# A decode attention kernel on one core: one 128-row load of keys is issued as six loads of 112, 3, 3, 3, 3 and 4 rows

## Chip, cores and metric

The kernel runs on one core of one Trainium2 chip. The metric is the time of one execution on the device, in microseconds (us), and lower is better. The time before is 1369.47 us, the median of three runs (1368.61 to 1370.11).

## What is computed

Two independent attention blocks are computed for one new token of each of four batches, and their outputs are laid side by side. Block A has 32 query heads that share 8 key and value heads, and looks at the last 2048 positions of its cache. Block B has 32 heads with keys and values of their own, and looks at all 8192 positions. All data are bf16, and the head dimension is 128.

```python
q = (x @ wq).reshape(B, Sq, H, Dh).transpose(0, 2, 1, 3)
scores = einsum("bhqd,bhkd->bhqk", q, k_cache) * (Dh ** -0.5)
p = softmax(scores, axis=-1)
o = einsum("bhqk,bhkd->bhqd", p, v_cache)
out = o.transpose(0, 2, 1, 3).reshape(B, Sq, H * Dh) @ wo
# A: the same, with the last W = 2048 positions and keys repeated 4 times
return concatenate([a, b], axis=-1)
```

Nearly all of the bytes are the keys and values of B: 4 batches x 32 heads x 8192 positions x 128 numbers of 2 bytes, twice, which is 537 MB of the 587 MB that are read in all.

## The kernel before, in words

The work is a list of chunks. The first eight (A, one for each key head) hold 64 tiles of 128 positions each for keys and as many for values. The next 32 (B, `NCA` = 8 to `NC` - 1) hold four heads of one batch: 256 key tiles and 256 value tiles of 128 x 128, that is 8 MB of keys and 8 MB of values a chunk. In SBUF a chunk's keys take 128 partitions of 64 KB each: one partition holds 256 consecutive positions of one head, and tile j is column block j of all partitions.

A chunk of B (`whole_B`) runs so: TensorE transposes eight key tiles at a time (a group g of 0 to 31, `emit_T`), VectorE or ScalarE copies the transposed group out of PSUM, TensorE multiplies it with the queries (`emit_S`), the softmax runs in two halves, and TensorE multiplies the probabilities with the values (`emit_pv`).

All loads but two tiny ones are issued by SyncE's queue (SP), one after another in the order in which `dma_kB`, `dma_vB`, `dma_wos` and their like are called: for each chunk of B the keys, then the values, and every fourth chunk the output weights ahead of them. Ahead of each load SP waits until the buffer that it overwrites has been read: keys for the transposes of the chunk before, values for the value products of the chunk before. `kpieces` and `vpieces` say into how many pieces a chunk's keys and values are cut by columns. The keys of B's first chunk (`ENDK`) come in three pieces of 64, 64 and 128 tiles, into different parts of the buffer: pieces 0 and 1 into the main part, where A's weights lay before, piece 2 into the spare part, which has to wait for A's last keys. Pieces 0 and 1 are each 128 rows (partitions) of 16 KB.

The landings are not waited for by TensorE itself. GpSimd's queue (POOL) waits for each piece's DMA semaphore in order (`land_kB`) and then raises a counter by the number of groups that came in; TensorE waits for that counter ahead of groups 0, 4, 8, 16 and 24 (`QK`, `QC`, `emit_T`). Piece 1 holds groups 8 to 15. Its semaphore belongs to B's first chunk alone.

The text below calls one of the core's 16 DMA engines a **lane**. A transfer is a list of rows; each row is one packet on one lane, and at its end every lane that took part sends one 4-byte packet that raises the semaphore.

Of the kernel before, what the change touches and what calls it, by code (L numbers as in the profile page):

```python
# [13 lines left out]
P = 128  # L14
# [3 lines left out]
NH = 10  # L18
NWO = 2
LATEWO = 2  # L20
LASTWO = 3
NPB = 2
NSM = 2
# [156 lines left out]
def bass_concat_heads__sliding_block_cached__mha_block_cached__decode_kernel(  # L180
# [30 lines left out]
    NCA = Hkv  # L211
# [13 lines left out]
    sch = _Sched()  # L225
    with ExitStack() as es:
# [5 lines left out]
        def ps(name, shape, dt):  # L232
# [72 lines left out]
            waits=["c_onesf", "c_identf"], key="c_ind")  # L305
# [39 lines left out]
        def flat(at, n):  # L345
            return kv[:, at:at + n, :].rearrange("p s x -> p (s x)")
# [4 lines left out]
        def dma_wq(ab, at):  # L351

            waits = take(("wq", ab), at, 2, ("qmm", ab))
            src = WQ[ab].rearrange("(p r) n -> p (r n)", r=KC)
            sch.add_dma("sp", lambda e: e.dma_start(flat(at, 2), src), "d_h%d" % at, waits=waits, key=("wq", ab))
# [4 lines left out]
        def dma_wo(g):  # L360

            src = A_wo[g * 4 * P:(g + 1) * 4 * P, :].rearrange("(p r) n -> p (r n)", r=4)
            slot = wo_slot(g)
            dst = wor[:, slot, :]
            if g == NCA - 1:
                for h, x in enumerate((slice(0, LASTWO * DO), slice(LASTWO * DO, 4 * DO))):
                    sch.add_dma("sp", lambda e, x=x: e.dma_start(dst[:, x], src[:, x]), "d_wos" if h else "d_wo%d" % slot,
                                waits=[] if h else [("fin", g - 2)], key=("wo", g, h))
                return
            sch.add_dma("sp", lambda e: e.dma_start(dst, src), "d_wo%d" % slot,  # L370
                        waits=[("fin", g - 2)] if g >= 2 else [], key=("wo", g))
# [16 lines left out]
        def kpieces(c):  # L388
            return ENDK if c == NCA else QUARTERS if c == NC - 1 else HALVES if c >= NC - NLATE else WHOLE
# [4 lines left out]
        def dma_kB(c):  # L394

            ch = chunks[c]
            src = B_k[ch["b"], 4 * ch["hq"]:4 * ch["hq"] + 4].rearrange("u (pp j) d -> (u pp) (j d)", pp=P // 4)
            pieces = kpieces(c)
            fam = "d_k%d_" % len(pieces)
            s0 = ch["s"] - ch["NG"]  # L400
            j0 = 0
            for i, n in enumerate(pieces):
                spare = len(pieces) > 1 and j0 >= KMAIN
                if spare:
                    dst = kspare[:, (j0 - KMAIN) * P:(j0 - KMAIN + n) * P]
                    waits = held[8] + held[9] if c == NCA else [("T", s0 + (j0 + n) // TG - 1)]
                else:
                    dst = flat(KB, 4)[:, j0 * P:(j0 + n) * P]
                    if c == NCA:
                        waits = held[0] + held[1] + held[2] + held[3]  # L410
                    else:
                        waits = [("T", s0 + min(j0 + n, KMAIN) // TG - 1)]
                        if j0 + n > KMAIN and len(kpieces(c - 1)) == 1:
                            waits += [("cp", c - 1)]
                x = slice(j0 * P, (j0 + n) * P)
                sch.add_dma("sp", lambda e, x=x, dst=dst: e.dma_start(dst, src[:, x]), fam + str(i), waits=waits, key=("k", c, i))
                j0 += n

        def land_kB(c):
# [24 lines left out]
        def dma_vB(c):  # L444

            ch = chunks[c]
            src = B_v[ch["b"], 4 * ch["hq"]:4 * ch["hq"] + 4].rearrange("u (pp j) d -> (u pp) (j d)", pp=P // 4)
            dst = flat(VB, 4)
            pieces = vpieces(c)
            fam = "d_v%d_" % len(pieces)  # L450
            j0 = 0
            for i, n in enumerate(pieces):
                waits = held[4] + held[5] + held[6] + held[7] if c == NCA else [("pv", c - 1, 0 if j0 + n <= NTB // 2 else 1)]
                x = slice(j0 * P, (j0 + n) * P)
                sch.add_dma("sp", lambda e, x=x: e.dma_start(dst[:, x], src[:, x]), fam + str(i), waits=waits, key=("v", c, i))
                j0 += n
# [21 lines left out]
        for c in range(NCA):  # L478
# [3 lines left out]
            if c == 2:  # L482
                dma_wq(1, 6)
            if c != 1 and c < NCA - LATEWO:
                dma_wo(c)
# [3 lines left out]
        for c in range(NCA, NC):  # L489
            if (c - NCA) % NB == 0:  # L490
                dma_wos((c - NCA) // NB)
            dma_kB(c)
            dma_vB(c)
        for c in range(NCA - LATEWO, NCA):
            dma_wo(c)
# [9 lines left out]
        def pe_mm(o, l, r, start=True, stop=True, transpose=False, waits=(), key=None):  # L505
            if transpose:
                sch.add("pe", lambda e: e.transpose(o, l, r), waits, key)  # L507
            else:
                sch.add("pe", lambda e: e.matmul(o, l, r, start=start, stop=stop), waits, key)  # L509
# [348 lines left out]
        def emit_fin(c):  # L858
            ab = 0 if c < NCA else 1
            if ab == 1:  # L860
                ov = oz[:, :].rearrange("p (b u) -> p b u", b=NB)
                ops = [(ov[:, :, u], wol[:, u, :]) for u in range(4)]
                waits = ["c_oz", ("oT", c)]
            else:
                w = wor[:, wo_slot(c), :].rearrange("p (r n) -> p r n", r=4)
                ops = [(zA[:, c % 2, r * NB:(r + 1) * NB], w[:, r, :]) for r in range(4)]
                waits = [("z", c), ("wo", c, 0) if c == NCA - 1 else ("wo", c)]

            for i, (l, r) in enumerate(ops):
                for h, (p0, x) in enumerate(out_halves(ab)):  # L870
                    pe_mm(fin[p0:p0 + NB, 0:DO // 2], l, r[:, x], start=False,
                          stop=i == len(ops) - 1 and c == NCA - 1,
                          waits=waits if i == h == 0 else [("wo", c, 1)] if c == NCA - 1 and (i, h) == (LASTWO, 0) else [],
                          key=("fin", c) if i == len(ops) - 1 and h == 1 else None)
# [172 lines left out]
        for p0, x in out_halves(1):  # L1047
            pe_mm(fin[p0:p0 + NB, 0:DO // 2], zz[:, :], sel4[:, 0:2, :].rearrange("p r x -> p (r x)"), start=False, key=("end", p0))
        for c in range(NCA - LATEWO, NCA - 1):
            emit_fin(c)  # L1050
# [61 lines left out]
```

## Time and profile before

| what | value |
|---|---|
| median of three runs | 1369.47 us |
| the profiled execution, its own time | 1369.16 us |
| span of the profiled execution (first to last instruction) | 1367.4 us |
| busiest engine, PE | 1221.8 us (89% of the span) |
| DMA packets, bytes, mean rate | 16773, 587.52 MB, 430 GB/s |

The profile's parts read as follows. The digits of its second part are busy shares in 40 equal slices of the span, and the GB/s row is what all lanes moved in each slice. The third part gives packets, bytes and busy share of each DMA queue; q1 is the queue of SP's loads, q10 that of ScalarE's (ACT's), q8 and q14 bring program code. The chain of work that ended last goes back from the last instruction: a DMA in it stands for the time from its issue to its landing, its own time in the queue included. A time "from issue to landing" therefore counts the loads ahead of it too.

### The profile page before, as it was taken

What the parts mean: (1) busy time and instruction counts of PE and PEld (TensorE: products, weight loads), DVE (VectorE), ACT (ScalarE), POOL (GpSimd) and SP (SyncE); (2) the same over time, 40 slices, a digit from 0 to 9 for tenths busy, and PEclk for the clock granted to TensorE, in tenths of its full rate; (3) what the DMA queues carried; (4) which work ended last, traced back from release to release, by engine and by line L of the source; (5) the groups of instructions that cost most, each with busy time, mean ns of one, the idle gap of its engine ahead of it and who ended that gap; (6) DMA issues with size and microseconds to landing.
All of it is one profiled execution on the core that took longest, in us unless ns stands there. A gap on an engine that the chain in (4) does not pass through costs nothing.

```text
span 1367.4 us, 62934 instructions
## 1 busy us (share of the span) xinstructions
PE 1221.8 (89%) x27807; PEld 1125.7 (82%) x27843; DVE 731.9 (54%) x1495; ACT 554.9 (41%) x777; POOL 202.8 (15%) x84
## 2 busy tenths in 40 slices
PE   6688799989898999888989899889899989899998
PEld 5587698878887988888889888878898888888888
DVE  3575355545455555454555555545555545455565
ACT  3353244434344443333444344334444333344443
POOL 2000022222210222222101222221012222200000
PEclk9898999999999999999999999999999999999999
DMA  9999999999999999999999999999999999999998
GB/s 399 427 427 429 434 438 429 433 437 418 435 433 435 429 437 429 437 429 437 431 432 433 435 424 435 437 431 431 433 435 433 433 430 439 437 424 430 429 427 370
DMA packets 16773, 587.52 MB, mean 430 GB/s; under 512 B 1880, under 2 KB 2032, under 8 KB 4208
## 3 DMA queue, kind: packets, MB, share of 16 engines
q1 hardware_dynamic: 16720, 587.21, 99.7%
q8 instruction: 15, 0.25, 0.1%
q14 instruction: 6, 0.05, 0.0%
q10 hardware_dynamic: 32, 0.01, 0.0%
HBM read 587.21 MB, written 0.01 MB: 429 GB/s over the span
## 4 chain that ended last, share of the span: by engine, by line
DMA 57%; PE 38%; issue 2%; DVE 2%; ACT 1%; SPq 0%; ACTq 0%; POOLq 0%; DVEq 0%
DMA kv<-in_B_k_cache_dram 51%; PE tr L507 22%; PE sc L509 10%; DMA kv<-in_A_k_cache_dram 4%; PE tr L509 3%; DMA kv<-in_B_v_cache_dram 2%; PE po L509 2%; PE ms L509 1%; DVE kt L584 0%; DVE sA L637 0%; PE fin L509 0%; ACT pba L736 0%; PE sc L940 0%; ACT pbb L706 0%; PE ms L507 0%
## 5 line engine op out<-in xcount | busy, mean ns | idle before, releaser
L507 PE MATMUL tr<-identb,kv 128*128 128x128 bf16 x8704 | 671.9, 223 | 50.0 <-POOLq L83 36.1
L584 DVE COPY kt<-tr 128x1024 bf16<-128x1024 bf16 x736 | 502.7, 691 | 318.9 <-PE tr L507 315.4
L507 PEld LDWEIGHTS tr<-identb,kv 128*128 128x128 bf16 x8704 | 521.0, 100 | 61.8 <-issue 54.3
L582 ACT ACTIVATE kt<-tr 128x1024 bf16<-128x1024 bf16 x352 | 359.3, 1023 | 455.2 <-PE tr L507 452.9
L509 PE MATMUL sc<-qq,kt 128*128 128x64 bf16 x8192 | 400.6, 192 | 11.1 <-DVE kt L584 9.4
L509 PEld LDWEIGHTS sc<-qq,kt 128*128 128x128 bf16 x8192 | 330.3, 98 | 17.7 <-DVE kt L584 12.7
L431 POOL COPY kv<-kv 128x4096 int32<-128x4096 int32 x54 | 192.9, 3602 | 988.6 <-DMA kv<-in_B_k_cache_dram 988.6
L706 ACT ACTIVATE pbb<-sc,negb 32x128 bf16<-32x128 f32 x256 | 137.8, 538 | 134.3 <-DVE negb L688 131.5
L509 PE MATMUL tr<-pbb,kv 128*128 128x64 bf16 x4096 | 135.7, 193 | 28.3 <-ACT pbb L706 25.4
L509 PEld LDWEIGHTS tr<-pbb,kv 128*128 128x128 bf16 x4096 | 131.0, 99 | 32.1 <-issue 30.0
L509 PE MATMUL po<-pbb,kv 128*128 128x64 bf16 x4096 | 135.0, 194 | 4.6 <-issue 4.6
L509 PEld LDWEIGHTS po<-pbb,kv 128*128 128x128 bf16 x4096 | 127.5, 98 | 5.6 <-issue 4.7
L854 ACT ACTIVATE wol<-tr 128x512 bf16<-128x512 f32 x32 | 19.1, 597 | 204.0 <-PE po L509 204.0
L856 DVE CAST wol<-tr 128x512 bf16<-128x512 f32 x64 | 41.2, 686 | 54.9 <-PE tr L509 54.9
L940 PE MATMUL sc<-sel,identb 128*128 128x512 bf16 x167 | 51.0, 384 | 13.5 <-issue 13.5
L940 PEld LDWEIGHTS sc<-sel,identb 128*128 128x128 bf16 x167 | 16.2, 97 | 48.4 <-issue 38.3
L713 DVE TENSOR_REDUCE rs<-pbb 128x4 f32<-128x512 bf16 x32 | 22.0, 686 | 50.0 <-ACT pbb L706 50.0
L786 DVE RECIPROCAL ib<-ms 128x8 f32<-128x8 f32 x32 | 6.6, 208 | 59.4 <-PE ms L509 59.4
L509 PE MATMUL tr<-wos,back 32*128 32x512 bf16 x384 | 34.8, 383 | 0.7 <-issue 0.5
L509 PE MATMUL po<-wos,back 32*128 32x512 bf16 x128 | 33.9, 384 | 0.0
L674 DVE TENSOR_REDUCE gm<-ms 4x4 f32<-4x128 f32 x72 | 19.8, 275 | 25.0 <-PE ms L507 25.0
L654 DVE TENSOR_REDUCE rh<-sc 128x4 f32<-128x512 f32 x32 | 22.1, 692 | 14.3 <-PE sc L509 14.3
(92 smaller groups left out, 505.4 us busy)
## 6 DMA issues: line engine op xcount, KB each, us to landing
kv<-in_B_v_cache_dram SPq DMA_DIRECT2D x10, 4096.0 KB, 24.0
kv<-in_B_k_cache_dram SPq DMA_DIRECT2D x7, 4096.0 KB, 19.7
kv<-in_A_k_cache_dram SPq DMA_DIRECT2D x8, 2048.0 KB, 15.7
kv<-in_A_v_cache_dram SPq DMA_DIRECT2D x8, 2048.0 KB, 16.6
kv<-in_B_k_cache_dram SPq DMA_DIRECT2D x6, 2048.0 KB, 26.2
kv<-in_B_v_cache_dram SPq DMA_DIRECT2D x3, 2048.0 KB, 30.0
kv<-in_A_wq_dram SPq DMA_DIRECT2D x1, 4096.0 KB, 12.3
kv<-in_B_wq_dram SPq DMA_DIRECT2D x1, 4096.0 KB, 23.0
```

Source lines behind the costliest of these rows:

```text
L431: sch.add("pool", lambda e, dst=dst, org=org: e.tensor_copy(dst, org), waits=[("T", s0 + ch["NG"] - 1)] if g == QC[0] else [])
L507: sch.add("pe", lambda e: e.transpose(o, l, r), waits, key)
L509: sch.add("pe", lambda e: e.matmul(o, l, r, start=start, stop=stop), waits, key)
L582: sch.add("act", lambda e: e.activation(dst, src, ACTF.Copy), waits=waits, key=("ev", s))
L584: sch.add("dve", lambda e: e.tensor_copy(dst, src), waits=waits, key=("ev", s))
L654: sch.add("dve", lambda e: e.tensor_reduce(out=dst, in_=src, axis=AX.X, op=ALU.max), waits=[("S", ch["s"] + (half + 1) * ch["NG"] // 2 - 1 ...
L674: sch.add("dve", lambda e: e.tensor_reduce(out=gm[0:C, m, 0:U], in_=src, axis=AX.X, op=ALU.max), waits=[key_of("trm", c, half)], key=key_o ...
L706: sch.add("act", lambda e, src=src, dst=dst, pp=pp, u=u: e.activation(dst, src, ACTF.Exp, bias=negb[pp, half, u:u + 1], scale=scale), wait ...
L713: sch.add("dve", lambda e: e.tensor_reduce(out=dst, in_=probs_of(c, half).rearrange("p j u -> p u j"), axis=AX.X, op=ALU.add), waits=[("ex ...
L854: sch.add("act", lambda e, u=u, o=o: e.activation(wol[:, u, :], o, ACTF.Copy), waits=[("reord", c, u)], key=("wol", c, u))
L856: sch.add("dve", lambda e, u=u, o=o: e.tensor_copy(wol[:, u, :], o), waits=[("reord", c, u)], key=("wol", c, u))
L940: return e.matmul(sc[:, 1, :], identb[:, :], sel4[:, :, :].rearrange("p r x -> p (r x)"), start=True, stop=True)
```

## The change

In `dma_kB`, piece 1 of B's first chunk of keys is no longer one transfer of 128 rows of 16 KB. It becomes six transfers of 112, 3, 3, 3, 3 and 4 rows, which together cover the same rows, source and destination, and are issued one behind the other in its place. The first one has the wait that the single one had; the others have none. All six raise the same semaphore, by 16 each, and the piece counts as landed when it has reached 96 in place of 16.

```diff
+UNEVEN = (112, 3, 3, 3, 3, 4)
...
                 x = slice(j0 * P, (j0 + n) * P)
-                sch.add_dma("sp", lambda e, x=x, dst=dst: e.dma_start(dst, src[:, x]), fam + str(i), waits=waits, key=("k", c, i))
+                r0 = 0
+                for rows in UNEVEN if (c, i) == (NCA, 1) else (P,):
+                    y = slice(r0, r0 + rows)
+                    r0 += rows
+                    sch.add_dma("sp", lambda e, x=x, y=y, dst=dst: e.dma_start(dst[y, :], src[y, x]), fam + str(i), waits=waits, key=("k", c, i) if r0 == P else None)
+                    waits = []
                 j0 += n
```

The one place where instructions move is SP's queue, between B's first output weights and its second chunk of keys. Before, SP issued this (each row is a line of the kernel, the tile written, the tensor read, and rows x elements; L377 are output weights, L416 keys and L455 values):

```order
L377 DMA wos<-in_B_wo_dram 128x2048
L416 DMA kv<-in_B_k_cache_dram 128x8192 x2
L416 DMA kv<-in_B_k_cache_dram 128x16384 [waits eng_pe]
L455 DMA kv<-in_B_v_cache_dram 128x16384 [waits eng_pe]
L455 DMA kv<-in_B_v_cache_dram 128x16384
L416 DMA kv<-in_B_k_cache_dram 128x32768 [waits eng_pe]
```

Now it issues this (the same lines are L378, L421 and L461):

```order
L378 DMA wos<-in_B_wo_dram 128x2048
L421 DMA kv<-in_B_k_cache_dram 128x8192
L421 DMA kv<-in_B_k_cache_dram 112x8192
L421 DMA kv<-in_B_k_cache_dram 3x8192 x4
L421 DMA kv<-in_B_k_cache_dram 4x8192
L421 DMA kv<-in_B_k_cache_dram 128x16384 [waits eng_pe]
L461 DMA kv<-in_B_v_cache_dram 128x16384 [waits eng_pe]
L461 DMA kv<-in_B_v_cache_dram 128x16384
L421 DMA kv<-in_B_k_cache_dram 128x32768 [waits eng_pe]
```

The second of the two 128x8192 loads has become six, all of them ahead of the load that waits for TensorE; every other row stands as it stood, and the other engines' instructions are the same.

## The prediction

> **What bounds the kernel now.** I read the profile's page first, and of it the DMA rows, then the stretches, then the queue that issues.
>
> ```profile
> DMA  9999999999999999999999999999999999999998
> GB/s 399 427 427 429 434 438 429 433 437 418 435 433 435 429 437 429 437 429 437 431 432 433 435 424 435 437 431 431 433 435 433 433 430 439 437 424 430 429 427 370
> ...
> q1 hardware_dynamic: 16720, 587.21, 99.7%
> q8 instruction: 15, 0.25, 0.1%
> ...
> q10 hardware_dynamic: 32, 0.01, 0.0%
> ...
> DMA 57%; PE 38%; issue 2%; DVE 2%; ACT 1%; SPq 0%; ACTq 0%; POOLq 0%; DVEq 0%
> ```
>
> The lanes are busy from the first slice to the last, and no slice stands out: SP's queue alone takes 99.7% of the time of 16 lanes. The chain calls only 57% of the span DMA, but PE's share there is work that runs while transfers run. The stretches say it without the chain (columns: stretch, its length, busy time of PE, PEld, DVE, ACT and POOL with instruction counts, granted clock, DMA share, GB/s):
>
> ```profile
> 180.00:400.00 220.00, 201.65 (x4629) 187.01 (x4631) 117.96 (x235) 89.78 (x126) 35.73 (x10) 0.98 1.00 432
> 400.00:1100.00 700.00, 637.90 (x14523) 586.50 (x14538) 374.96 (x735) 284.82 (x396) 128.64 (x36) 0.98 1.00 433
> 1100.00:1360.00 260.00, 242.61 (x5631) 225.36 (x5633) 145.79 (x287) 110.62 (x153) 21.44 (x6) 0.99 1.00 429
> ```
>
> DMA share 1.00 in all three: no lane has time to spare, so **the bound is bytes per lane**, and a stretch ends when its fullest lane is through. 433 GB/s over 16 lanes is 27.06 GB/s each. A row of 16 KB (16384 B) takes a lane 0.605 us, and a whole transfer of 128 such rows, eight to a lane, 4.84 us.
>
> The loads are issued early enough for that. These are SP's rows around one chunk, and two pieces of the chain for the same loads:
>
> ```profile
> 259.31 0.33 SPq L416 DMA_DIRECT2D kv<-in_B_k_cache_dram  x1
> 281.24 0.33 SPq L455 DMA_DIRECT2D kv<-in_B_v_cache_dram  x1
> 300.67 0.33 SPq L416 DMA_DIRECT2D kv<-in_B_k_cache_dram  x1
> 322.61 0.33 SPq L455 DMA_DIRECT2D kv<-in_B_v_cache_dram  x1
> ```
>
> ```profile
> 259.31 29.25 DMA kv<-in_B_k_cache_dram
> ...
> 300.67 26.59 DMA kv<-in_B_k_cache_dram
> ```
>
> Keys land at 288.56 and 327.26, 38.70 us apart for 16 MB. The values behind the second are issued at 322.61, when 4.65 us of the keys ahead are still to come: that is the thinnest queue here. A lane that lags never runs out; one that is over 4.65 us ahead of the last does, and waits.
>
> **What the change takes away, adds and moves.** The execution profiled took 1369.16 us, 0.31 us below the median of the runs; I sum against it.
>
> The bytes are the same. What may differ is how many rows a lane carries. The profile doesn't number the lanes, but it counts packets. ACT's queue, q10, holds four transfers of four rows (two loads of x, two stores), and 32 packets: eight each, four rows and four ends. So a four-row transfer runs on four lanes, not on 16. I take a three-row transfer to run on three, the 112-row one on all 16 with seven rows each, and the narrow ones always on the same first lanes; no row says which lanes these are. Lanes 0 to 2 then hold 7 + 4 + 1 = 12 of these rows in place of 8, lane 3 holds 8, lanes 4 to 15 hold 7. [...]
>
> Now the **price of four rows more** on three lanes. The trace has no narrow transfer of 16 KB rows, so I bound it.
> - Below: if the narrow rows were dealt to a new set of lanes each time, 16 rows on 16 lanes make 7 + 1 = 8 for each, and the price is nothing; were lanes 0 to 2 well ahead of the others, the end would come earlier by the row that the others lost, 0.6 us.
> - In the middle: three lanes move three rows at once, at 0.605 us a row. Lanes 0 to 2 are 4 x 0.605 = 2.4 us late, the others 0.6 us early.
> - Above: three lanes that write into neighbouring partitions get no more than one lane's 27 GB/s together. Then the 16 rows pass one at a time, and lanes 0 to 2 are through after 7 + 16 = 23 row times in place of 8: 15 x 0.605 = 9.1 us late. If, on top, the 112-row transfer's lanes, whose rows no longer match the eight-to-a-lane layout, get in each other's way, its seven rows at half rate add 7 x 0.605 = 4.2 us: 13.3 us.
>
> I take 9.1 us. The rate of 433 GB/s is only ever seen in transfers over all 128 partitions, where each lane has eight partitions of its own; nothing in the trace shows several lanes going at 27 GB/s each into partitions that lie side by side, and 112 to 114, 115 to 117 and so on do. [...]
>
> **What hides part of it.** The lanes aren't level. Program code is loaded beside the data:
>
> ```profile
> q8 instruction: 8, 0.13, 0.8%
> ...
> kv<-in_B_k_cache_dram SPq DMA_DIRECT2D x1, 34.2
> ```
>
> This is the stretch from 110 to 180 us (its last row, an issue of keys with its time to landing, is used below): 0.8% of 16 x 70 us over 8 packets is 1.1 us each, and each falls on one lane. The other seven of the page's 15 came earlier. A lane that was spared twice is 2.2 us ahead of one that was hit twice. Lanes 0 to 2 may be ahead by 0 to 2.2 us, and the last of the three counts: I take 1.1 us, which leaves **9.1 - 1.1 = 8.0 us**.
>
> **The other instructions.** Here is the issue of the three pieces, and what the same line shows by itself in that stretch:
>
> ```profile
> 99.45 0.59 SPq L377 DMA_DIRECT2D wos<-in_B_wo_dram  x1
> 100.09 6.29 SPq L416 DMA_DIRECT2D kv<-in_B_k_cache_dram  x3
> 120.11 0.80 SPq L455 DMA_DIRECT2D kv<-in_B_v_cache_dram  x2
> 136.82 0.33 SPq L416 DMA_DIRECT2D kv<-in_B_k_cache_dram  x1
> ```
>
> ```profile
> L416 SPq DMA_DIRECT2D kv<-in_B_k_cache_dram x3: 327/432/432, 100.1 to 106.1; - x3
> ...
> DMA to landing us min/median/max: 16.0/20.4/25.8
> ```
>
> Three issues of at most 0.43 us stand in 6.29 us; the third waits for TensorE until 106.1. Five more issues, 5 x 0.43 = 2.2 us, fit into that wait; without it they would delay every load behind them, which even then are 25.8 us from landing. Nothing.
>
> Piece 1 was issued at about 100.5, right behind piece 0, and landed 20.4 us later, at 120.9. GpSimd's queue waits for it as before, only for 96. TensorE comes to group 8, piece 1's first, here:
>
> ```profile
> 128.91 0.61 PE L507 MATMUL tr<-identb,kv 128*128 128x128 bf16 x8
> 129.36 0.40 PE L509 MATMUL sc<-qq,kt 128*128 128x64 bf16 x8
> 129.59 0.61 PE L507 MATMUL tr<-identb,kv 128*128 128x128 bf16 x8
> ...
> 136.18 0.61 PE L507 MATMUL tr<-identb,kv 128*128 128x128 bf16 x8 [1.66 <-issue]
> 136.62 0.40 PE L509 MATMUL sc<-qq,kt 128*128 128x64 bf16 x8
> 136.86 0.55 PE L507 MATMUL tr<-identb,kv 128*128 128x128 bf16 x7
> ```
>
> Groups 7, 8, 15 and 16 start at 128.91, 129.59, 136.18 and 136.86. With 8 us more, piece 1 comes at 128.9, still in time; piece 2, which landed at 106.1 + 25.8 = 131.9, comes at 139.9, 3 us after group 16 wants it. That wait of 3 us delays the transposes, and with them SP's next waits, but the load that SP issues at 136.82 has 34.2 us to landing, so the queue stays full. The cost is in the lanes, not in TensorE.
>
> Behind this point nothing is made good: every later transfer has the same rows for every lane, so the lag stays to the end. The others, 9.7 us ahead, run dry at the thin points of the queue (4.65 us) and wait; that costs nothing while lanes 0 to 2 are last.
>
> Sum: 1369.16 + 8.0 = **1377.2 us**.
>
> **Rivals.**
> 1. *Lanes alone* (the middle price): +2.4 us less a cover of 0 to 2.2 us gives +0.2 to +2.4, 1369.4 to 1371.6 us. For it: all that is seen of a lane is its own 27 GB/s. Against it: only the argument of the neighbours.
> 2. *More than one at a time*: +9.1 to +13.3 us, 1378.3 to 1382.5 us, if the 112 rows suffer as well. For it: seven rows to a lane can't fall on eight partitions each. Against it: it takes a second mechanism.
> 3. *The other side: levelling.* If three lanes go at full rate and lanes 0 to 2 are well ahead, they take on 2.4 us that cost nothing, while the lanes that end last lose a row each. From a lead of 2.4 us on the kernel is faster, from 3.0 us (2.4 + 0.6) on by the whole row, 0.6 us: 1368.6 to 1369.4 us. For it: program loads alone can give a lead of 2.2 us. Against it: that isn't 2.4, and 15 program packets on 16 lanes will hardly have spared all three.
> 4. *The change doesn't do what it says*: narrow transfers are dealt round the lanes. The price is nothing, 1369.2 us; I count it with the third.
>
> **How the numbers follow.** Forecast (one at a time, 7 to 9.1 us): 0.57. Rival 2: 0.07. Rival 1: 0.26. Rivals 3 and 4: 0.10. The range goes from the low end of rival 1, 1369.4, to the top of rival 2, 1382.5, and leaves out the 0.10. A measurement can tell some 0.2% from no change, 2.7 us: slower by more than that are the forecast, rival 2 and a little of rival 1 (0.02), 0.65; faster by more has no mechanism here, 0.02; within it 0.33.
>
> **What the profile of the changed kernel would show.** Packets of q1: 16720 + 16 = 16736 (128 + 16 + 4 x 3 + 4 ends for 128 + 16) if three rows take three lanes. The time from issue to landing of the 4096 KB piece of keys: 25.8 us before, some 34 us if the rows pass one at a time, 28 with lanes alone. The DMA share from 180 to 400 us: 12 or 13 lanes that drop a lead of 9.7 us to some 4.65 us wait 5 us each, 65 of 3520 lane us, so 0.98 in place of 1.00; by rival 1 it stays at 1.00. TensorE waits some 3 us ahead of group 16. The forecast is wrong if the landing is less than 4 us later, or if the lag that is there at 140 us isn't there any more at the end.

## The result and the profile after

| | before | after |
|---|---|---|
| median (lowest to highest), six runs each | 1369.54 us (1368.61 to 1370.93) | 1376.90 us (1376.36 to 1377.94) |
| ratio, 95% interval | | 1.0058 [1.0048, 1.0068] |
| the profiled execution: time, span | 1369.16, 1367.4 us | 1377.94, 1376.2 us |

The kernel is slower by 7.4 us on the medians, 0.58%. The profiled execution is the slowest of its six, 1.0 us above their median, so the two traces stand 8.8 us apart. That is the difference to be accounted for below.

The page of the kernel after first, with its DMA rows (40 equal slices, then packets, megabytes and share of the 16 lanes' time for each queue):

```profile
DMA  9999999999999999999999999999999999999998
GB/s 399 427 428 332 433 431 442 415 439 430 430 429 440 429 430 440 434 432 431 436 429 434 432 429 430 440 425 430 442 432 436 432 427 429 440 429 429 432 426 365
DMA packets 16789, 587.52 MB, mean 427 GB/s; under 512 B 1896, under 2 KB 2048, under 8 KB 4224
...
q1 hardware_dynamic: 16736, 587.21, 99.7%
```

The digits are the same as before: 9, that is 90% or more, in every slice but the last. But the fourth slice, about 103 to 138 us, moved 332 GB/s in place of 429. **Busy is not the same as moving**: the lanes' packets took longer there. The stretches show where (columns: stretch, its length, busy time of PE, PEld, DVE, ACT and POOL, granted clock, DMA share, GB/s). The kernel after:

```profile
110.00:180.00 70.00, 50.04 (x1014) 44.99 (x1013) 27.31 (x64) 19.27 (x30) 0.00 (x0) 0.82 1.01 382
112.00:124.00 12.00, 8.05 (x182) 7.33 (x182) 3.23 (x15) 2.33 (x6) 0.00 (x0) 0.60 1.07 269
112.00:122.00 10.00, 7.35 (x174) 6.91 (x170) 3.23 (x15) 2.33 (x6) 0.00 (x0) 0.62 1.09 287
116.00:120.00 4.00, 3.98 (x66) 3.82 (x66) 0.26 (x1) 0.21 (x1) 0.00 (x0) 0.50 1.02 233
122.00:132.00 10.00, 8.32 (x119) 6.42 (x120) 4.57 (x7) 3.14 (x4) 0.00 (x0) 0.70 0.95 234
124.00:128.00 4.00, 3.67 (x29) 2.23 (x23) 1.77 (x3) 1.09 (x2) 0.00 (x0) 0.50 0.99 193
124.00:132.00 8.00, 7.62 (x115) 6.00 (x108) 4.57 (x7) 3.14 (x4) 0.00 (x0) 0.74 0.93 248
180.00:400.00 220.00, 203.69 (x4631) 189.12 (x4637) 121.33 (x233) 91.65 (x124) 42.87 (x12) 0.98 1.00 433
400.00:1100.00 700.00, 638.07 (x14470) 586.79 (x14485) 372.90 (x734) 285.54 (x396) 128.64 (x36) 0.98 1.00 432
```

The kernel before, for some of these stretches:

```profile
110.00:180.00 70.00, 55.63 (x1216) 50.77 (x1215) 32.89 (x73) 23.30 (x34) 7.14 (x2) 0.90 1.01 431
112.00:122.00 10.00, 8.26 (x186) 7.42 (x186) 3.29 (x16) 2.32 (x6) 0.00 (x0) 0.63 1.02 434
112.00:124.00 12.00, 9.93 (x196) 8.04 (x194) 4.21 (x18) 3.18 (x8) 0.00 (x0) 0.61 1.03 438
122.00:132.00 10.00, 9.67 (x181) 8.27 (x175) 6.40 (x10) 4.16 (x5) 0.00 (x0) 0.86 1.01 431
124.00:132.00 8.00, 8.00 (x169) 7.66 (x168) 5.49 (x9) 3.30 (x4) 0.00 (x0) 0.95 0.99 424
```

The loss is in one place. From 110 to 180 us (431 - 382) x 70 us = 3.4 MB fewer came in, 7.9 us at 433 GB/s; from 180 us on the rate is the old one. Inside that stretch the two parts of the changed piece are told apart by the order in which SP issues them: first the 112 rows, then the 16 narrow rows. No view shows which part a packet belongs to, so the cut is an estimate. Cut at 124 us, (438 - 269) x 12 / 433 = **4.7 us** are lost ahead of it and (433 - 248) x 8 / 433 = **3.4 us** behind it; cut at 122 us, (434 - 287) x 10 / 433 = 3.4 us and (431 - 234) x 10 / 433 = 4.5 us. About half of the loss, then, belongs to the 112 rows, which use all 16 lanes (by the 16736 packets of q1, which hold 16 ends for them), and they move 233 GB/s from 116 to 120 us at a DMA share of 1.02, where they are alone or nearly so.

The other half is not a matter of three lanes either. From 124 to 128 us the DMA share is 0.99, so all lanes have packets; if only three lanes were slow, the other 13 would move 13 x 27.06 = 352 GB/s, but all together move 193. **All 16 lanes are slow together while the narrow rows move.** Which lanes carry these rows no view shows; if it is the few that the forecast took, the others are held up by rows that they don't carry. (Some of the 112 rows may still run at the start of this stretch; e9 below shows the same without them.)

That the lanes do not stand still in the first of the two is seen in their packets. From 112 to 124 us, after:

```profile
DMA packets 215, 3.23 MB, mean 269 GB/s; under 512 B 27, under 2 KB 27, under 8 KB 27
q1 hardware_dynamic: 214, 3.21, 106.4%
```

and before:

```profile
DMA packets 286, 5.26 MB, mean 438 GB/s; under 512 B 32, under 2 KB 32, under 8 KB 32
...
q1 hardware_dynamic: 285, 5.24, 102.3%
```

A quarter fewer packets and 39% fewer bytes fill as much lane time. (A share above 100% is a matter of the count: a packet counts whole in the stretch in which it starts. From 112 to 124 us the share is 1.07, from 124 to 132 us 0.93, and over both 1.01.)

The lag then stays to the end. SP's rows of the kernel after, its issues of this piece and of the loads further on (start, time, line, tile and tensor), with the landing times of the first group behind them:

```profile
99.98 6.32 SPq L421 DMA_DIRECT2D kv<-in_B_k_cache_dram  x8
120.01 1.88 SPq L461 DMA_DIRECT2D kv<-in_B_v_cache_dram  x2
139.55 0.33 SPq L421 DMA_DIRECT2D kv<-in_B_k_cache_dram  x1
...
269.56 0.33 SPq L421 DMA_DIRECT2D kv<-in_B_k_cache_dram  x1
...
307.99 0.33 SPq L421 DMA_DIRECT2D kv<-in_B_k_cache_dram  x1
```

```profile
L421 SPq DMA_DIRECT2D kv<-in_B_k_cache_dram x8: 240/312/432, 100.0 to 105.9; - x8
...
DMA to landing us min/median/max: 17.6/26.4/35.1
```

The last of the eight issues is the 4096 KB piece 2. It lands 35.1 us after 105.9, at 141.0; before, 25.8 us after 106.1, at 131.9. That is 9.1 us later. The chain gives the two loads that the forecast looked at further on, and the last one:

```profile
269.56 27.82 DMA kv<-in_B_k_cache_dram
307.99 28.09 DMA kv<-in_B_k_cache_dram
...
1335.46 34.19 DMA kv<-in_B_v_cache_dram
```

These land at 297.38, 336.08 and 1369.65 us, against 288.56, 327.26 and, by the last row of the same view of before,

```profile
1327.51 33.32 DMA kv<-in_B_v_cache_dram
```

1360.83. The lag is 8.8, 8.8 and 8.8 us: nothing is made good and nothing is added after 140 us.

TensorE's rows about group 16, the first of piece 2, in the kernel after (start, time, what, and in brackets the idle time ahead of it and what ended it):

```profile
136.75 0.61 PE L513 MATMUL tr<-identb,kv 128*128 128x128 bf16 x8
138.91 0.61 PE L513 MATMUL tr<-identb,kv 128*128 128x128 bf16 x8 [1.32 <-issue]
141.14 0.62 PE L513 MATMUL tr<-identb,kv 128*128 128x128 bf16 x8 [1.39 <-POOLq L84]
```

TensorE waits 1.39 us for the counter that piece 2 raises, and starts group 16 at 141.14, 4.3 us later than the 136.86 of before.

### The profile page after: what moved, and what is told of

It reads as the page before. It is cut to its first block, busy times and chain, and to the rows that moved or that the text cites. A ratio compares the mean times of both kernels' runs of the same rounds, so it can differ in the third digit from the quotient of the medians.

```text
span 1376.2 us, 62939 instructions
## 1 busy us (share of the span) xinstructions
PE 1226.5 (89%) x27807; PEld 1129.9 (82%) x27843; DVE 731.9 (53%) x1495; ACT 556.6 (40%) x777; POOL 202.8 (15%) x84
## 2 busy tenths in 40 slices
DMA packets 16789, 587.52 MB, mean 427 GB/s; under 512 B 1896, under 2 KB 2048, under 8 KB 4224
## 3 DMA queue, kind: packets, MB, share of 16 engines
q1 hardware_dynamic: 16736, 587.21, 99.7%
## 4 chain that ended last, share of the span: by engine, by line
DMA 58%; PE 38%; issue 2%; DVE 2%; ACT 1%; SPq 0%; ACTq 0%; POOLq 0%; DVEq 0%
DMA kv<-in_B_k_cache_dram 51%; PE tr L513 22%; PE sc L515 10%; DMA kv<-in_A_k_cache_dram 4%; PE tr L515 3%; DMA kv<-in_B_v_cache_dram 2%; PE po L515 1%; PE ms L515 1%; DVE sA L643 0%; PE fin L515 0%; PE sc L946 0%; DVE kt L590 0%; ACT pbb L712 0%; ACT pba L742 0%; PE ms L513 0%
## 5 line engine op out<-in xcount | busy, mean ns | idle before, releaser
L515 PEld LDWEIGHTS tr<-pbb,kv 128*128 128x128 bf16 x4096 | 131.9, 100 | 31.7 <-issue 29.3
L946 PEld LDWEIGHTS sc<-sel,identb 128*128 128x128 bf16 x167 | 16.2, 97 | 48.4 <-issue 38.3
```

The costliest lines, as they stand in the source:

```text
L946: return e.matmul(sc[:, 1, :], identb[:, :], sel4[:, :, :].rearrange("p r x -> p (r x)"), start=True, stop=True)
```

## The experiments

Three theories stood against each other. **A**, the forecast's: neighbouring partitions share a path that is no faster than one lane, so it counts which partitions are written at the same time. **B**: each lane goes at its own 27 GB/s into any partition, and only its number of rows counts. **C**: each further transfer has a fixed cost. All three are the author's guesses: no view shows a path or its rate, and what A says of lanes and paths is its own assumption throughout. Ratios are against the kernel before, run beside the experiment on the same chip; its medians were 1368.83 us for e1 to e4, 1368.81 for e5 to e8 and 1368.74 for e9 to e12. Except where a line says so, only the cut of piece 1 differs. Code that is left out is marked with `...`; `parts` lists the slices of rows that become transfers, for the piece that is cut alone, and the loop over it is the one shown for e8.

### e1: the 112 rows and one transfer of 16

```diff
-UNEVEN = (112, 3, 3, 3, 3, 4)
+UNEVEN = (112, 16)
```

> The same rows in two transfers of 112 and 16, so that every lane carries eight rows again (7 + 1). Theory A (partitions that lie side by side share a path that is no faster than one lane, so the 112 rows, seven neighbours to a lane, run at half rate, and 16 rows on 16 lanes share the paths of four): 7 x 0.6 = 4.2 us for the 112 rows and 3 x 0.6 = 1.8 us for the 16, less some cover: +4 to +6 us. Theory B (only the rows per lane count): nothing, within 0.5 us. Theory C (each further transfer costs the same, 7.4 us / 5 = 1.5 us): +1.5 us.

Measured: 1375.37 us (1374.89 to 1376.99), ratio 1.0049 [1.0035, 1.0062], 6.5 us. There is no narrow transfer left here: both parts run on 16 lanes (16736 packets on q1, 16 more than before, are one further set of 16 ends), with 7 + 1 = 8 rows each if the rows are dealt evenly, as in the single transfer. By B this costs nothing; A's +4 to +6 us is a little low, though the interval, 4.8 to 8.5 us, reaches into it. Its stretches:

```profile
112.00:124.00 12.00, 7.87 (x186) 7.39 (x189) 3.42 (x16) 2.33 (x6) 0.00 (x0) 0.72 1.04 265
124.00:132.00 8.00, 7.64 (x122) 5.93 (x116) 4.57 (x7) 3.13 (x4) 0.00 (x0) 0.79 0.98 336
```

The first is that of the change (265 against 269 GB/s); the second loses (433 - 336) x 8 / 433 = 1.8 us in place of 3.4. So most of the change's price, 6.5 of 7.4 us, comes without its narrow transfers.

### e2 and e8: two halves, by blocks and by every second row

e2:

```diff
+UNEVEN = (64, 64)
```

> Two transfers of 64 rows, four rows to a lane in each, eight in all. Theory A: each half reaches half of the paths and takes 4.8 us in place of 2.4 us: +4.8 us, the same on all lanes. Theory B: nothing, within 0.5 us. Theory C: +1.5 us.

e8:

```diff
-                sch.add_dma("sp", lambda e, x=x, dst=dst: e.dma_start(dst, src[:, x]), fam + str(i), waits=waits, key=("k", c, i))
+                parts = (slice(0, P, 2), slice(1, P, 2)) if (c, i) == (NCA, 1) else (slice(0, P),)
+                for k, y in enumerate(parts):
+                    sch.add_dma("sp", lambda e, x=x, y=y, dst=dst: e.dma_start(dst[y, :], src[y, x]), ...)
...
```

> Two transfers of the even rows and of the odd rows, 64 each. [...] Theory A, if the lanes take their rows as in a whole transfer (each from its own path): nothing, within 0.7 us. Theory A, if a lane takes four rows that follow each other in the transfer (8e, 8e + 2, 8e + 4, 8e + 6): lanes e and e + 4 want the same path at the same time, +4 to +6.6 us as with plain halves. Theory B: nothing.

Measured: e2 1375.46 us (1374.73 to 1376.65), ratio 1.0049 [1.0036, 1.0063], 6.6 us, where A had +4.8 us, just below the interval's 4.9; e8 1368.69 us (1368.33 to 1370.48), ratio 1.0001 [0.9992, 1.0011], nothing. Both kernels issue two transfers of 64 rows on 16 lanes (each has 16736 packets on q1, 16 ends more than before), with the same bytes. In e2 one writes partitions 0 to 63 and the other 64 to 127; in e8 each writes every second one. e2 while it moves the halves:

```profile
116.00:120.00 4.00, 3.88 (x66) 3.87 (x66) 0.32 (x2) 0.34 (x2) 0.00 (x0) 0.50 1.03 225
120.00:124.00 4.00, 1.75 (x23) 0.81 (x20) 0.86 (x5) 0.00 (x0) 0.00 (x0) 0.50 1.03 225
```

and e8 from 112 to 124 us:

```profile
112.00:124.00 12.00, 10.08 (x211) 8.73 (x208) 4.92 (x18) 3.41 (x8) 0.00 (x0) 0.72 1.03 440
```

225 GB/s is half of 433 (0.52), and 440 is full rate. The pair parts the theories without any narrow transfer: the number of transfers, of lanes and of rows per lane are equal, and what differs is which partitions are written together. This is the plainest evidence for A, and B and C have no place for it. Two things limit it. The rows of the key cache that are read together differ in the same way, and no run here parts the reading side from the writing side. And A had two forms for e8, by how a lane takes its rows; the one with lanes that meet on a path had +4 to +6.6 us and fails.

### e3: six transfers, cut by columns

```diff
+                    cuts = (0, 11, 22, 33, 44, 54, 64)
+                    for k in range(6):
+                        y, z = slice(cuts[k] * P, cuts[k + 1] * P), slice((j0 + cuts[k]) * P, (j0 + cuts[k + 1]) * P)
...
+                        sch.add_dma("sp", lambda e, z=z, y=y, dst=dst: e.dma_start(dst[:, y], src[:, z]), ...)
...
```

> Six transfers again, but cut by columns: each has all 128 rows and 10 or 11 of the 64 tiles (2560 or 2816 B a row). Theory A: nothing beyond the shorter rows, within 1 us. Theory B: the same. Theory C: +7.4 us.

Measured: 1368.86 us (1368.65 to 1369.96), ratio 1.0000 [0.9991, 1.0009]. Six transfers of 128 rows cost nothing, although their rows are 2.5 to 2.75 KB in place of 16 KB. C falls, and with it any cost of SP's five further issues.

### e5, e6 and e7: who gets the narrow rows

All three have 112 rows in one transfer and 16 rows in four transfers of four. In e5 each four are neighbours, at the top; in e6 each takes every fourth of the top 16; in e7 the 112 are partitions 16 to 127, and each four are every fourth of partitions 0 to 15.

```diff
+UNEVEN = (112, 4, 4, 4, 4)                                                       # e5
+parts = (slice(0, 112),) + tuple(slice(112 + k, P, 4) for k in range(4)) ...     # e6
+parts = (slice(16, P),) + tuple(slice(k, 16, 4) for k in range(4)) ...           # e7
```

> 112 rows and then four transfers of four neighbouring rows (112 to 115, 116 to 119, and so on), each on four lanes. Theory A (neighbours share a path that is no faster than one lane): the four rows of a transfer pass at the speed of one lane, and its path is also wanted by the lane that owns it: as the change itself, +7 to +8 us. Theory B (rows per lane alone, beside the 112 rows at half rate that the 112 and 16 cut showed): three rows more on four lanes, 1.8 us, in place of nothing: also some +7 us. This run is the base of the next two.

> The same rows and sizes as 112 and four times 4, but each of the four small transfers takes every fourth row (112, 116, 120, 124, then 113, 117, ...), so that its four lanes write to four different paths. Theory A: a row shares its path with the owning lane only, two at a time in place of four or five: some 4 x 0.6 = 2.4 us less than with neighbours, +4 to +6 us. Theory B: the same time as with neighbours, within 0.5 us.

> One transfer of rows 16 to 127 (112 rows) and four of every fourth row of 0 to 15 (0, 4, 8, 12, then 1, 5, 9, 13, ...). [...]

| | time (lowest to highest) | ratio, 95% interval | over before |
|---|---|---|---|
| e5 neighbours | 1377.20 us (1376.73 to 1380.55) | 1.0067 [1.0053, 1.0081] | 8.4 us |
| e6 every fourth of 112 to 127 | 1376.69 us (1376.29 to 1376.87) | 1.0058 [1.0044, 1.0071] | 7.9 us |
| e7 every fourth of 0 to 15 | 1375.36 us (1374.55 to 1377.20) | 1.0049 [1.0035, 1.0063] | 6.6 us |

The stretch from 124 to 132 us, in which the narrow rows move, first e5, then e6, then e7:

```profile
124.00:132.00 8.00, 7.67 (x117) 6.13 (x110) 4.22 (x7) 2.97 (x4) 0.00 (x0) 0.71 0.93 283
```

```profile
124.00:132.00 8.00, 7.67 (x128) 6.11 (x122) 4.60 (x7) 3.13 (x4) 0.00 (x0) 0.79 0.95 319
```

```profile
124.00:132.00 8.00, 7.67 (x136) 6.11 (x130) 4.98 (x8) 3.13 (x4) 0.00 (x0) 0.84 0.98 389
```

The rates of the change, e5 and e6 stand in A's order: 248 GB/s in the change and 283 in e5 for neighbours, 319 spread. e7 has 389, and no run shows why rows 0 to 15 do better than rows 112 to 127. The times of e5, e6 and e7 stand in the same order, but the intervals of the ratios overlap, and the expectations were met in part only: e6 is above A's +4 to +6 us and within 0.5 us of e5, which is what B had. So at 16 KB rows these times do not part A from B for the narrow rows. And the size is not the forecast's: if 16 rows passed one at a time, e5 would be far above e6. It is 0.5 us above. Beyond e1's 112 and 16, at 6.5 us, the narrow transfers add 0 to 2 us.

### e9: narrow rows without the 112

```diff
+                parts = tuple(slice(k, P, 4) for k in range(3)) + tuple(slice(k + 3, k + 16, 4) for k in range(0, P, 16)) if (c, i) == (NCA, 1) else (slice(0, P),)
...
```

Three transfers of 32 rows over all partitions, and eight of four rows, each over 16 neighbouring partitions.

> No transfer of 112 rows here: three transfers of every fourth row (32 rows, over all paths, as the even rows that cost nothing), and the last fourth in eight transfers of four rows (3, 7, 11, 15, then 19, 23, 27, 31 and so on), each on four lanes, its rows on four paths. Four lanes carry 6 + 8 = 14 rows, the others 6. Theory B (rows per lane alone): 6 more, 3.6 us, less a cover of 0 to 2.2 us: +1.4 to +3.6 us. Theory A (paths): seven of the eight small rows of a lane share a foreign path two at a time, 7 x 0.6 = 4.2 us on top: +5.6 to +7.8 us.

Measured: 1376.88 us (1375.13 to 1378.63), ratio 1.0061 [1.0047, 1.0075], 8.1 us, or 6.4 to 10.3 by the interval: above B's figure, and in the median 0.3 us above A's range. Eight narrow transfers cost as much as the whole change, without any block of 112 rows. Its stretches, and then those of the kernel before:

```profile
112.00:118.00 6.00, 5.10 (x137) 4.90 (x138) 2.60 (x11) 2.33 (x6) 0.00 (x0) 0.70 1.06 442
118.00:128.00 10.00, 8.83 (x138) 6.78 (x137) 4.61 (x11) 2.11 (x3) 0.00 (x0) 0.67 1.01 279
```

```profile
112.00:118.00 6.00, 5.10 (x139) 4.91 (x136) 2.44 (x11) 2.32 (x6) 0.00 (x0) 0.71 1.00 423
118.00:128.00 10.00, 8.83 (x134) 6.79 (x133) 4.59 (x11) 2.11 (x3) 0.00 (x0) 0.66 1.03 441
```

Until 118 us, while piece 0 and the 32-row transfers behind it move, nothing is lost: 442 GB/s. Behind it, with the narrow rows, (441 - 279) x 10 / 433 = 3.7 us go at a DMA share of 1.01. If only four lanes were slow, the other twelve would move 12 x 27.06 = 325 GB/s at their own rate, so here too the lanes are slow together. The execution profiled took 6.0 us more than the one before; the other 2.3 us come behind 128 us and are not explained here.

### e4, e10, e11 and e12: the same cuts at rows of 64 KB

These cut the keys of B's second chunk, one transfer of 128 rows of 64 KB, and leave piece 1 whole. At the rate of the kernel before, a row now takes 4 x 0.605 = 2.42 us, an estimate. e4 has the change's cut, e10 112 and 16, e11 112 and four times four neighbours, e12 112 and four times every fourth. The diff of e4 is against the kernel after, the others are against the kernel before.

```diff
-                for rows in UNEVEN if (c, i) == (NCA, 1) else (P,):
+                for rows in UNEVEN if (c, i) == (NCA + 1, 0) else (P,):                  # e4
...
+parts = (slice(0, 112), slice(112, P)) ...                                           # e10
+parts = (slice(0, 112),) + tuple(slice(k, k + 4) for k in range(112, P, 4)) ...      # e11
+parts = (slice(0, 112),) + tuple(slice(k, P, 4) for k in range(112, 116)) ...        # e12
```

> The cut into 112, 3, 3, 3, 3 and 4 rows is taken from this piece (rows of 16 KB) and put on the whole keys of B's second chunk (rows of 64 KB, one transfer before). Theory A: all row times are four times as long, so 4 x 7.4 to 4 x 9 = +30 to +36 us, less nothing. Theory B: 4 x 2.4 = +9.7 us less a cover of 1 to 2 us: +8 us. Theory C: as in the change, +7.4 us.

> As the run with the cut on the whole keys of B's second chunk (64 KB rows, +48.4 us), but in two transfers of 112 and 16 rows. If the 112 rows at half rate are most of that cost: what the narrow rows add is four times the difference seen in the small piece, 4 x 0.8 to 4 x 1.6 = 3 to 6 us, so +42 to +45 us. If the narrow rows pass one at a time, as I forecast: 4 x (9.1 - 1.8) = 29 us less, +19 us.

> The same place, 112 rows and four times four neighbouring rows. Theory A: four rows of 64 KB on one path at a time, +46 to +50 us, and 4 x 0.5 to 4 x 2.4 = 2 to 10 us more than with the four rows of a transfer on four paths. Theory B: the same as that, within 2 us.

> The same place, 112 rows and four transfers of every fourth row of 112 to 127, so that the four rows of a transfer go to four paths. Theory A: 2 to 10 us less than with four neighbours, +38 to +46 us. Theory B: the same as with neighbours, within 2 us.

| | time (lowest to highest) | ratio, 95% interval | over before |
|---|---|---|---|
| e4: 112, 3, 3, 3, 3, 4 | 1417.26 us (1415.62 to 1419.04) | 1.0358 [1.0342, 1.0374] | 48.4 us |
| e10: 112, 16 | 1397.01 us (1394.17 to 1397.38) | 1.0199 [1.0183, 1.0214] | 28.3 us |
| e11: 112, four neighbours x 4 | 1422.43 us (1419.02 to 1423.83) | 1.0383 [1.0367, 1.0399] | 53.7 us |
| e12: 112, every fourth x 4 | 1399.37 us (1398.94 to 1401.75) | 1.0228 [1.0213, 1.0244] | 30.6 us |

e12 and e11 have the same numbers of transfers, rows and lanes, and differ by 23.1 us, far over both intervals: it matters which rows move together, as A says and B and C do not. A's sizes were off: e4 and e11 are above its ranges (+30 to +36, +46 to +50), e12 is below (+38 to +46). The stretch from 190 to 215 us, e11 first, then e12, for which the stretch ahead of it is shown as well:

```profile
190.00:215.00 25.00, 0.00 (x0) 0.00 (x0) 0.00 (x0) 0.00 (x0) 0.00 (x0) 0.50 1.01 104
```

```profile
180.00:195.00 15.00, 1.82 (x22) 0.69 (x19) 1.29 (x2) 1.08 (x2) 0.00 (x0) 0.70 0.95 198
190.00:215.00 25.00, 14.42 (x267) 14.43 (x268) 8.09 (x12) 5.12 (x5) 7.14 (x2) 0.67 0.86 290
```

In e11 the DMA share is 1.01 and the rate 104 GB/s: all 16 lanes have packets, and on the mean each moves 104 / 16 = 6.5 GB/s, a quarter of its 27.06. e12, while its narrow rows move (180 to 195 us), has 198 GB/s at a share of 0.95, a little under half of 433. By A four neighbours share a path in e11, and in e12 a narrow row shares one with the lane that owns it: a quarter and a half are A's factors. But here they are the rates of all 16 lanes together, while a transfer of four rows runs on four (q10's 32 packets for four such transfers). That A did not say, and why it is so no run here shows.

By e10 the 112 rows with an even rest cost 28.3 us of e4's 48.4; the narrow cut adds 20.1. The result of e10 lies between the two figures expected, +42 to +45 and +19 us. It is close to four times e1 (4 x 6.5 = 26 us), while the narrow cut's 20.1 us are far more than four times the 0.9 us that lie between e1 and the change.

A part of the size in e4 cannot be scaled down, because here TensorE does run dry (PE is idle in all of e11's 25 us) and the queue with it. SP issues the next keys at 181.69 us before, but at 228.75 in e4, and until they come the lanes run empty. The row of e4:

```profile
215.00:240.00 25.00, 23.63 (x492) 23.50 (x493) 15.07 (x24) 12.28 (x14) 7.14 (x2) 0.89 0.58 240
```

A DMA share of 0.58 is lanes without work: (1 - 0.58) x 25 = 10.5 us of those 48.4. In the change itself that doesn't happen; its share is 0.93 and more in every stretch shown.

## Why the prediction was right in its total, and where it was not

The forecast of 1377.2 us stands 0.3 us from the measured 1376.90. **The total came out by two wrong terms that nearly cancel, and that is luck**; step by step:

1. *The bound is bytes per lane.* Half right. The lag of 140 us goes through to the end undiminished, as said. But the DMA share was read as proof that lanes move at their rate; in the change it is 1.02 while they move 233 GB/s (116 to 120 us).
2. *The rows per lane.* The packets came as counted: 16736 on q1, 16 more than before, and the packets under 512 B rose by the same 16, from 1880 to 1896, so the six transfers sent 32 ends, which is 16 for the 112 rows and one for each narrow row: three rows run on three lanes and four on four. That these are always the same lanes was an assumption, which no run shows.
3. *The price of the narrow rows, 9.1 us, on lanes 0 to 2.* **This is the term that was mis-sized.** In the trace their stretch lost 3.4 to 4.5 us, by where it is cut, and 1.8 of the 3.4 remains in e1, where the 16 rows go in one transfer on 16 lanes. That it matters which rows move together is shown by e2 against e8 (6.6 us and nothing) and by e11 against e12 (53.7 and 30.6 us). That three lanes into neighbouring partitions get no more than one lane's 27 GB/s, so that 16 rows pass one at a time for 9.1 us, no run shows: e5 and e6 lie 0.5 us apart and e1 only 0.9 us below the change. And the path was wrong: the forecast made three lanes late and left the others 9.7 us ahead, but from 124 to 128 us all lanes were held up together, at 193 GB/s.
4. *The 112 rows at nothing.* Wrong: they run at 233 GB/s, and their stretch lost 3.4 to 4.7 us. The upper bound had this, as "seven rows at half rate", with 4.2 us, and gave it to rival 2 with a chance of 0.07. So about half of the loss is the second mechanism that rival 2 asked for; rival 2's time, 1378.3 us and more, was missed only since the narrow rows cost less than it had.
5. *The cover of 1.1 us.* Not tested. Throughput lost sums to 4.7 + 3.4 = 8.1 us against 8.8 us of span, so there is nothing left that a cover would have to explain.
6. *SP's five further issues at nothing.* Right: eight issues stand in 6.32 us, where three stood in 6.29, and e3 measures nothing for six transfers.
7. *TensorE waits 3 us ahead of group 16.* Right in place, half in size: 1.39 us. The landing at 141.0 us is 1.1 us later than forecast, but TensorE had slipped as well: it starts group 15 at 138.91 us in place of 136.18.
8. *The DMA share from 180 to 400 us, 0.98.* Failed: it is 1.00, which the forecast had given as the sign of rival 1. If all 16 lanes are slowed alike, as 233 GB/s at a share of 1.02 and 193 at 0.99 suggest, none gets 9.7 us ahead, and none runs dry. The check could not tell rival 1 from that, and read alone it would have pointed to the wrong theory.

Of the two signs by which the forecast was to be wrong neither came: the landing took 9.3 us longer (35.1 against 25.8), and the lag was still there at the end. Both look the same whichever rows cause the lag, so they could not show that half of it was the 112 rows'.

Rival 1, lanes alone, falls to e1 and e2, which by the same count have eight rows on each lane and cost 6.5 and 6.6 us; rivals 3 and 4, no change or a faster kernel, fall with the result.

What stays open: why the 112 rows go at half rate (they write 112 different partitions, and no view shows which lane writes which at what moment); whether what is shared lies where the rows are written or where they are read; which lanes carry the narrow rows, and why all 16 are slow together while they move; and why neighbours cost 23.1 / 4 = 5.8 us for each 16 KB of row in e11 against e12, but only 0.5 us in e5 against e6. Lanes that run dry cannot be all of that last difference, since e11 moves 104 GB/s at a share of 1.01.

## What to carry to other kernels

Where a kernel lives off the DMA rate, cut a load by columns, or into halves of every second row (both measured at nothing: ratios 1.0000 in e3 and 1.0001 in e8), and not by blocks of rows: even 64 and 64, with every lane in use, ran at 225 GB/s. Transfers of a few rows are dear by themselves: eight of four rows cost 8.1 us in e9. A busy share of DMA near 1.00 says only that lanes have packets; divide the bytes by the time, stretch by stretch, before calling it full rate. And a forecast that hits its total still needs its terms measured one by one: here one term was at least twice too large and another was left at zero.

## What was not expected of the hardware

- 112 rows on 16 lanes, seven to a lane on the mean, move at 233 GB/s, hardly faster than 64 rows of one half (225), though they leave out only an eighth of the partitions.
- Two transfers of 64 rows, each over every second partition, are as fast as one of 128 rows: 440 GB/s, ratio 1.0001.
- Lanes that are held up show as busy: a DMA share of 1.02 goes with 233 GB/s in the change, one of 1.01 with 104 GB/s in e11.
- While transfers of three and four rows move, all 16 lanes are slow together: 193 GB/s in the change at a share of 0.99.
- Four neighbouring rows of 64 KB at a time held the whole core to 104 GB/s for 25 us, and cost 53.7 us; the same rows four apart 30.6.
